# Attention with a mixture of experts on one core: the transposes between the second-layer products, and weight chunks in two DMAs

## The chip, the core and the metric

The kernel runs on one core of one Trainium2 chip. The metric is the device time of one execution in microseconds (us), as the median of several runs. Five engines work side by side, each on its own list of instructions: TensorE (PE) multiplies and transposes, VectorE (DVE), ScalarE (ACT) and GpSimd (POOL) do the elementwise work, and SyncE (SP) issues DMAs. They wait for one another by semaphores only.

## The reference

Block-causal attention over 8 batches of 8 heads, 576 rows and 64 columns, and then a layer of eight experts, of which each of the 4608 rows uses one.

```python
scores = scale * np.matmul(q, k.transpose(0, 1, 3, 2))
mask = block_i >= block_j                      # blocks of 64 rows
attn = softmax(np.where(mask, scores, -1e9))
x = np.matmul(attn, v)                         # rearranged to 4608 x 512

logits = x @ w_gate                            # 512 x 8
expert_idx = np.argmax(logits, axis=1)
gate_w = softmax(logits)[np.arange(N), expert_idx]
for e in range(E):                             # 8 experts
    mask = expert_idx == e
    h = np.maximum(x[mask] @ w1[e], 0.0)       # w1[e]: 512 x 1024
    out[mask] = gate_w[mask, None] * (h @ w2[e])   # w2[e]: 1024 x 512
```

All of it is float32. The kernel reaches that accuracy by splitting each operand into a high part and the rest and adding three products: high by high, rest by high, high by rest.

## The kernel before, in words

The first 370 us or so are attention with the routing behind it; the change doesn't touch them. The rest is the class `Experts`. The rows are sorted by expert into slots of 128 rows (38 of them here; three early slots, 0 to 2, are prepared before the others). A slot's way is:

- `gather(t)`: POOL issues an indirect DMA that fetches the slot's 128 rows into `xg`.
- `rows_in(t)`: PE transposes them, four 128 x 128 tiles, into `px` (L895). `rows_act(t)`: ACT copies `px` twice, to `xh` (rounded, L905) and to `xf` (L908). `rows_pool(t)`: POOL makes the rest `xl` (L914).
- `first_pe(t)`: 24 first-layer products (L936), 12 into each of the two banks `ph`; the second bank shows in the trace under the name `o`.
- The hidden rows of the two banks are transposed in two ways. For bank 0, ACT splits the 32-bit words into two planes of 16 bits (`planes`, L983), issues a DMA transpose (`turned`, L995), puts the planes together again when it has landed (`joined`, L1001), and applies the ReLU twice, to `hh` and to `h[0]` (`joined_high`, L1009 and L1010). For bank 1, ACT applies the ReLU (`relu_act(t,1)`, L974), PE transposes four tiles into `pt` (`hidden_pe(t,1)`, L1018), and ACT copies them twice (`hidden_act`, L1028 and L1031). POOL makes the rest of both (`hidden_low`, L1037).
- `second_pe(t, part)`: 24 second-layer products (L1057) into `py`, 12 in each part.
- `out_act(t)`: ACT scales the result by the gate (L1074), and `out_pool(t)`: POOL scatters it to the output by an indirect DMA (L1081).

`period(t)` is one turn of the loop, from slot 2 to slot 37. It is written once and gives every engine its instructions in this order; an engine takes only its own. On PE an ordinary turn is: `first_pe(t)`, `rows_in(t+1)`, `hidden_pe(t,1)`, then `second_pe(t-1, 0)` and `second_pe(t-1, 1)`. So the second layer of a slot runs one turn after its first. On ACT it is: `out_act(t-2)`, `planes(t)`, `turned(t)`, `relu_act(t,1)`, `rows_act(t+1)`, `hidden_act(t,1)`, `joined(t)`, `joined_high(t)`. On POOL: `out_pool(t-2)`, `gather(t+2)`, `rows_pool(t+1)`, `hidden_low(t,1)`, `hidden_low(t,0)`. `planes(t+1)` waits for `hidden_low(t,0)`, since both use `h[0]`.

The turn of slot 2 is different: there PE has all of slot 0's second layer (24 products) before `hidden_pe(2,1)`, and `rows_in(3)` with `rows_act(3)` stands between the two parts of slot 1's second layer, so that in ACT's list `rows_act(3)` comes behind `joined(2)` and `joined_high(2)`.

The weights of the next expert come while the present one works. SP loads chunks of 512 KB into five buffers `raw` (`load`, L1176): four chunks of w1, with 4 KB for each of 128 partitions, and four of w2, with two runs of 2 KB for each. Before a load beyond the fifth SP waits until DVE has used up the buffer. DVE splits each chunk into its high part (`high`, L1183) and its rest (`low`, L1189), four chunks at a time, when the buffer of the expert before last is free.

Of the kernel before, what the change touches and what calls it, by code (L numbers as in the profile page):

```python
# [18 lines left out]
P = 128  # L19
# [773 lines left out]
class Experts:  # L793
# [40 lines left out]
    def chunk(self, row, c):  # L834

        if c < 4:
            return self.w1.rearrange("e d f -> (e d) f")[bass.ds(row + P * c, P), :]
        w2 = self.w2.rearrange("e f d -> (e f) d")[bass.ds(row * 2 + 2 * P * (c - 4), 2 * P), :]
        return w2.rearrange("(k p) d -> p k d", p=P)

    def parts(self, e, c):

# [3 lines left out]
    def run(self):  # L846
        nc, tc, NS = self.nc, self.tc, self.nslot
        raw = self.raw
        nr = len(raw)
# [38 lines left out]
        def rows_in(t):  # L888

            if t >= EARLY:  # L890
                pe.wait_ge(sg[t % 4], 16 * gathered(t))
            if t >= 2:
                pe.wait_ge(sem["xa"], 2 * t - 2)
            for k in range(4):
                m = pe.transpose(self.px[:, P * k : P * k + P], self.xg[t % 4][:, P * k : P * k + P], self.ident)  # L895
                if t == 1 and k < 2:

                    m.then_inc(sem[("mm1", "mm2")[k]], (3, 1)[k])
            m.then_inc(sem["xt"], 1)
# [139 lines left out]
        def second_pe(t, part):  # L1039
            e8, off = self.regs[t]  # L1040
            todo = [
                (h[t % 2], base, c) for h, base in ((self.hh, 8192), (self.hl, 8192), (self.hh, 12288)) for c in range(8)
            ]
            if part == 0:
                pe.wait_ge(sem["wh"], e8 + 8 if t >= EARLY else 4)
                pe.wait_ge(sem["ha"], 4 * t + 3)
                if t >= 2:
                    pe.wait_ge(sem["ya"], t - 1)
            for n in range(12 * part, 12 * part + 12):
                h, base, c = todo[n]  # L1050
                if n == 8:
                    pe.wait_ge(sem["hp"], 2 * t + 2)
                if t == 0 and n >= 16 and c % 2 == 0:
                    pe.wait_ge(sem["wd"], 5 + c // 2)
                elif n == 16:
                    pe.wait_ge(sem["wd"], e8 + 8)
                m = pe.matmul(  # L1057
                    self.py[t % 2],
                    h[:, c // 4, P * (c % 4) : P * (c % 4) + P],
                    wf[:, bass.ds(off + (base + 512 * c), 512)],  # L1060
                    start=n == 0,
                    stop=n == 23,
                )
            if part == 1:
                m.then_inc(sem["mm2"], 1)
# [46 lines left out]
        def period(t):  # L1112
            more = t + 1 < NS
            if t > 2:
                first_pe(t)
                out_act(t - 2)
            planes(t)
            turned(t)
            relu_act(t, 1)
            if t == 2:  # L1120

                for f in range(2):
                    second_pe(0, f)
                out_act(0)
            elif more:
                rows_in(t + 1)
                rows_act(t + 1)
            hidden_pe(t, 1)
            hidden_act(t, 1)
            joined(t)  # L1130
            joined_high(t)
            for f in range(2):
                second_pe(t - 1, f)
                if t == 2 and f == 0:
                    rows_in(t + 1)
                    rows_act(t + 1)
            out_pool(t - 2)
            if t + 2 < NS:
                gather(t + 2)
            if more:  # L1140
                rows_pool(t + 1)
            for f in (1, 0):
                hidden_low(t, f, pool)
# [18 lines left out]
        with tc.tile_critical():  # L1162
            done = 0

            def do(m):

                nonlocal done
                done += 1
                m.then_inc(sem["do"], 1)
                dve.wait_ge(sem["do"], done)  # L1170

            def load(m, row):

                c = (m + 4) % 8
                dst = raw[m % nr] if c < 4 else raw[m % nr].rearrange("p (k d) -> p k d", k=2)
                sp.dma_start(dst, self.chunk(row, c)).then_inc(sraw[m % nr], 16)  # L1176

            def high(m):
                e, c = divmod(m + 4, 8)
                hi, _ = self.parts(e, c)  # L1180
                if m >= 4:
                    dve.wait_ge(sraw[m % nr], 16 * (m // nr + (m % nr == 4)))
                dve.tensor_copy(hi, raw[m % nr]).then_inc(sem["wh"], 1)  # L1183

            def low(m):
                e, c = divmod(m + 4, 8)
                hi, lo = self.parts(e, c)
                dve.wait_ge(sem["wh"], m + 5 if m >= 4 else 4)
                dve.tensor_sub(lo, raw[m % nr], hi).then_inc(sem["wd"], 1)  # L1189


            posi, g, cnt = self.router.rest
            last, t0 = self.router.B - 1, self.out.shape[0] - S
            sp.dma_start(
                self.router.by_partition(last, 3 * P, DM), self.y.rearrange("p (i c) -> p i c", c=P)
            ).then_inc(sem["ga"], 16)
            sp.dma_start(self.router.by_partition(last, GATE, GATE + 1), g[:, 0:4, None]).then_inc(sem["ga"], 16)
            sp.dma_start(self.xd[t0 : t0 + 64, GATE : GATE + 1], g[0:64, 4:5]).then_inc(sem["ga"], 16)
            begin()
            for i in range(5):  # L1200
                if i == 1:
                    rows_pool(1)
                self.router.scatter(last, i, posi).then_inc(sem["sc"], 16)
            rows_pool(2)
            gather(EARLY)
            for k in range(4):
                m = dve.tensor_copy(tuple(self.parts(0, k))[1], self.low[k].rearrange("p a b -> p (a b)"))
            m.then_inc(sem["lc"], 1)

            dve.wait_ge(sem["lc"], 1)  # L1210
            dve.sem_inc(sem["wd"], 4)
            for m in range(4):
                high(m)
            self.router.slots(cnt, do, self.bank)
            dve.sem_inc(sem["me"], 1)
            for f in range(2):
                hidden_low(0, f, dve)
            for f in range(2):
                low(2 * f)
                low(2 * f + 1)  # L1220
                hidden_low(1, f, dve)
            for f in range(2):
                o = slice(2048 * f, 2048 * f + 2048)
                dve.tensor_copy(self.w[:, 0, 0, o], self.high[:, o]).then_inc(sem["wh"], 2)
            sp.wait_ge(sem["sc"], 80)
            sp.dma_start(self.stab, self.router.tabv).then_inc(sem["st"], 16)

            sp.wait_ge(sem["me"], 1)
            sp.wait_ge(sem["mm1"], 2 * EARLY + 1)
            for e in range(1, E):  # L1230
                row = sp.value_load(self.row[e : e + 1, 0:1], min_val=0, max_val=DM * (E - 1))
                for c in range(8):
                    m = 8 * e + c - 4
                    if m >= nr:
                        sp.wait_ge(sem["wd"], m)
                    load(m, row)
                if e >= 2:
                    before = dve.value_load(self.before[e - 1 : e, 0:1], min_val=0, max_val=NS)
                for half, name, of in ((0, "mm1", lambda: before * 2 + 1), (4, "mm2", lambda: before + 1)):
                    if e >= 2:  # L1240
                        dve.wait_ge(sem[name], of())
                    for part in (high, low):
                        for c in range(half, half + 4):
                            part(8 * e + c - 4)
            total = None

            def tail(t):
                if t == NS:
                    finish(NS - 1)
                    return  # L1250
                with nc.If(total > t):
                    period(t)
                    tail(t + 1)
                with nc.Else():
                    finish(t - 1)

            for t in range(2, least):
                period(t)
            if least < NS:
                act.wait_ge(sem["me"], 1)  # L1260
                total = nc.values_load(self.before[E : E + 1, 0:1], min_val=0, max_val=NS)
                tail(least)
            else:
                finish(NS - 1)
# [129 lines left out]
```

## Time and profile before

| | us |
|---|---|
| median of 3 runs | 877.45 |
| lowest and highest run | 871.00, 880.23 |
| the profiled execution | 871.89 |
| its span in the trace | 870.1 |

The profile shows one execution, and its span is 1.8 us shorter than its time. An engine's busy time is that of its instructions; register, branch and semaphore work isn't counted. A line such as `L1018 PE MATMUL pt<-ident,h` names the line of the kernel, the engine, the operation, and the tile written and the tiles read. PEld is TensorE's loading of weights, which overlaps its products. ACTq and SPq are the DMA issues of ACT and SP. In a timeline the columns are the start, the duration of the group, engine, line, operation, and in brackets the idle time of the engine before it and what ended it.

The costliest groups of the page are these (busy us, then the mean ns of one, then the idle time before them):

```profile
L1057 PE MATMUL py<-w,low 128*128 (+1 forms) x912 | 224.2, 402 | 0.0
...
L936 PE MATMUL ph<-w,xh 128*128 x280 | 76.6, 396 | 2.1 <-ACT xh L905 2.1
L936 PE MATMUL o<-w,xh 128*128 x280 | 75.8, 393 | 0.0
```

The DMA issues of the weight chunks, with their size and the median time from issue to landing:

```profile
raw<-w SPq DMA_DIRECT2D x60, 512.0 KB, 5.3
```

Four of those 60 are loads of the first expert during attention, by another line; the other 56 are by `load`.

### The profile page before, as it was taken

The numbers are of one execution on the slowest core, as the hardware profiler recorded it, in microseconds if no ns is written. First come the engines' busy times: TensorE is split into PE (matmuls) and PEld (weight loads), VectorE is DVE, ScalarE is ACT, GpSimd is POOL, SyncE is SP. The second block draws the span as 40 slices with busy tenths as digits, with TensorE's granted clock in tenths as the row PEclk, the third lists the DMA queues.
The fourth block names the chain that finished last, engine by engine and source line by source line (L and its number), as shares of the span: only waits on it lengthen the run. The fifth ranks groups of instructions, "written<-read, shape, count | busy, mean of one in ns | idle before, by whom it ended". The sixth has DMA issues, their size and how long they took to land.

```text
span 870.1 us, 16492 instructions
## 1 busy us (share of the span) xinstructions
PE 825.4 (95%) x5126; PEld 633.9 (73%) x5126; DVE 425.8 (49%) x1208; ACT 555.1 (64%) x1254; POOL 352.4 (41%) x390
## 2 busy tenths in 40 slices
PE   5999999999999999998998999998998799999997
PEld 4777767777777777676876877786777577777775
DVE  5778787878787877478034000158256343000000
ACT  6889888888888888444554455444544444555453
POOL 2000223232323412445554545456556355554453
PEclk8999999999999999999999999999999899999999
DMA  5234748363635353528427422259557752122222
GB/s 196 96 112 152 153 130 168 118 157 114 148 116 142 107 132 122 129 53 262 154 74 173 132 59 74 74 134 249 155 147 225 170 138 70 48 74 74 59 51 64
DMA packets 83707, 108.81 MB, mean 125 GB/s; under 512 B 45601, under 2 KB 48929, under 8 KB 83618
## 3 DMA queue, kind: packets, MB, share of 16 engines
q1 hardware_dynamic: 38082, 78.26, 31.3%
q0 software_dynamic: 7520, 19.97, 7.9%
q10 hardware_dynamic: 38016, 9.44, 6.7%
q8 instruction: 50, 0.82, 0.4%
q14 instruction: 39, 0.32, 0.1%
HBM read 76.76 MB, written 21.98 MB: 113 GB/s over the span
## 4 chain that ended last, share of the span: by engine, by line
PE 77%; issue 6%; ACT 6%; POOL 2%; DMA 2%; ACTq 1%; POOLq 1%; DVE 1%; DVEq 0%
PE py L1057 20%; PE o L304 10%; PE ph L936 10%; PE o L936 9%; PE o L339 4%; PE ya L202 3%; PE xa L202 3%; PE pt L1018 2%; ACT h L974 2%; PE yb L202 2%; DMA kd<-kT 2%; ACTq L995 1%; PE o L333 1%; POOLq L1079 1%; ACT pb L234 1%
## 5 line engine op out<-in xcount | busy, mean ns | idle before, releaser
L1057 PE MATMUL py<-w,low 128*128 (+1 forms) x912 | 224.2, 402 | 0.0
L1057 PEld LDWEIGHTS py<-w,low 128*128 128x128 f32 x912 | 171.0, 191 | 37.7 <-issue 0.3
L1183 DVE CAST w<-raw 128x1024 fp32r<-128x1024 f32 x60 | 50.0, 880 | 206.8 <-PE o L936 154.3
L1037 POOL TENSOR_TENSOR low<-h,low 128x512 fp32r<-128x512 f32 x72 | 105.6, 1468 | 62.9 <-ACT h L1010 62.5
L247 POOL TENSOR_SCALAR p<-p,rs 128x64 f32<-128x64 f32 x32 | 14.2, 443 | 257.2 <-DVE rs L243 154.8
L1189 DVE TENSOR_TENSOR w<-raw,w 128x1024 fp32r<-128x1024 f32 x60 | 87.2, 1510 | 0.0
L914 POOL TENSOR_TENSOR xl<-xf,xh 128x512 fp32r<-128x512 f32 x38 | 51.1, 1346 | 86.6 <-ACT xf L908 86.4
L983 ACT COPY h<-ph 128x1024 uint16<-128x1024 uint16 x36 | 36.5, 1013 | 69.8 <-PE ph L936 61.3
L936 PE MATMUL ph<-w,xh 128*128 x280 | 76.6, 396 | 2.1 <-ACT xh L905 2.1
L936 PE MATMUL o<-w,xh 128*128 x280 | 75.8, 393 | 0.0
L1001 ACT COPY h<-hf 128x1024 uint16<-128x1024 uint16 x36 | 43.0, 1193 | 48.7 <-DMA hf<-h 48.5
L1081 POOL DMA_INDIRECT out<-y,idx x35 | 42.7, 1220 | 63.3 <-ACT y L1074 52.1
L936 PEld LDWEIGHTS ph<-w,xh 128*128 128x128 f32 x280 | 53.1, 190 | 14.6 <-issue 2.5
L974 ACT ACTIVATE h<-o 128x512 f32<-128x512 f32 x37 | 22.1, 598 | 63.4 <-PE o L936 54.7
L1074 ACT ACTIVATE y<-py,xg 128x512 f32<-128x512 f32 x38 | 26.1, 686 | 56.0 <-PE py L1057 54.5
L936 PEld LDWEIGHTS o<-w,xh 128*128 128x128 f32 x280 | 52.7, 188 | 11.7
L234 ACT ACTIVATE pb<-ya,neg 128x320 f32<-128x320 f32 (+2 forms) x93 | 48.6, 533 | 2.5 <-PE pt30x L273 1.8
L234 ACT ACTIVATE pb<-yb,neg 128x320 f32<-128x320 f32 (+2 forms) x93 | 49.5, 547 | 0.0
L731 POOL DMA_INDIRECT tab<-toks,posi x40 | 41.7, 1042 | 15.1 <-issue 14.6
L1018 PE MATMUL pt<-ident,h 128*128 128x128 f32 x152 | 25.1, 290 | 23.1 <-ACT h L974 23.1
L339 PE MATMUL o<-fold,oT 128*128 128x144 f32 x256 | 45.4, 300 | 0.9 <-ACT oT L311 0.6
L219 DVE TENSOR_REDUCE neg<-ya 128x1 f32<-128x320 f32 (+2 forms) x93 | 44.8, 482 | 0.8 <-ACT pb L234 0.8
(965 smaller groups left out, 2137.7 us busy)
## 6 DMA issues: line engine op xcount, KB each, us to landing
raw<-w SPq DMA_DIRECT2D x60, 512.0 KB, 5.3
qd<-qT SPq DMA_DIRECT2D x32, 352.0 KB, 3.0
v<-vt SPq DMA_DIRECT2D x32, 352.0 KB, 4.7
kd<-kT SPq DMA_DIRECT2D x32, 288.0 KB, 3.4
xd<-xt SPq DMA_DIRECT2D x7, 1026.0 KB, 11.6
xd<-xg SPq DMA_DIRECT2D x9, 256.5 KB, 6.5
xg<-w SPq DMA_DIRECT2D x8, 256.0 KB, 6.2
xd<-x SPq DMA_DIRECT2D x8, 128.0 KB, 6.2
```

Source lines behind the costliest of these rows:

```text
L202: ins = mm(out, q[x][r, 128 * (i - 1) : 128 * i], q[y][r, o : o + w], start=n == 0, stop=n == 2, skip_group_check=True,)
L219: ins = self.nc.vector.tensor_reduce(self.neg[m][:, c : c + 1], src, AX.XY if i == 4 else AX.X, ALU.max, negate=True)
L234: ins = self.nc.scalar.activation(dst, src, AF.Exp, bias=self.neg[m][:, c : c + 1], scale=1.0, accum_out=self.sums[m][:, c : c + 1])
L304: self.nc.tensor.matmul(out[r], self.raws[m][2][:, slot], self.ph[m, bank][:, c0:c1], start=t in (0, 5), stop=t in (4, 5), skip_group_chec ...
L339: mm(t[:, i], self.oT[m, 0][:, o : o + P], w, start=True, stop=True)
L914: pool.tensor_sub(self.xl, self.xf, self.xh).then_inc(sem["xp"], 1)
L936: m = pe.matmul(self.ph[f], x[:, P * k : P * k + P], weights(k, f, part), start=start and k == 0, stop=stop and k == 3,)
L1001: act.copy(self.h[0].bitcast(U16).rearrange("p (c o) -> p c o", o=2), self.hf.bitcast(U16).rearrange("p (o c) -> p c o", o=2),).then_inc(s ...
L1037: engine.tensor_sub(hl, self.hf if t < 2 else self.h[f], hh).then_inc(sem["hp"], 1)
L1057: m = pe.matmul(self.py[t % 2], h[:, c // 4, P * (c % 4) : P * (c % 4) + P], wf[:, bass.ds(off + (base + 512 * c), 512)], start=n == 0, st ...
L1183: dve.tensor_copy(hi, raw[m % nr]).then_inc(sem["wh"], 1)
L1189: dve.tensor_sub(lo, raw[m % nr], hi).then_inc(sem["wd"], 1)
```

## The change

Two things are changed. In `period`, the first part of the second-layer products of slot t-1 moves ahead of `rows_in(t+1)` and `hidden_pe(t,1)`, and the second part stays behind them, so that PE's eight transposes stand between the two parts. In the turn of slot 2 this puts `rows_in(3)` and `rows_act(3)` behind the first part of slot 1's second layer and ahead of `hidden_pe(2,1)` and `hidden_act(2,1)`.

In `load`, each chunk is taken as two halves of the columns, b = 0 and 1, each by its own DMA. The chunk is seen as 2 x 2 x 256 numbers for each partition, and a DMA carries two runs of 256 numbers (1 KB) for each. The bytes land where they did before. Each DMA adds 16 to the buffer's semaphore, so the count that DVE waits for is doubled.

```diff
     def chunk(self, row, c):
         if c < 4:
-            return self.w1.rearrange("e d f -> (e d) f")[bass.ds(row + P * c, P), :]
+            w1 = self.w1.rearrange("e d f -> (e d) f")[bass.ds(row + P * c, P), :]
+            return w1.rearrange("p (k b d) -> p k b d", k=2, b=2)
         w2 = self.w2.rearrange("e f d -> (e f) d")[bass.ds(row * 2 + 2 * P * (c - 4), 2 * P), :]
-        return w2.rearrange("(k p) d -> p k d", p=P)
+        return w2.rearrange("(k p) (b d) -> p k b d", p=P, b=2)
...
                 for f in range(2):
                     second_pe(0, f)
                 out_act(0)
-            elif more:
+            second_pe(t - 1, 0)
+            if more:
                 rows_in(t + 1)
                 rows_act(t + 1)
             hidden_pe(t, 1)
             hidden_act(t, 1)
             joined(t)
             joined_high(t)
-            for f in range(2):
-                second_pe(t - 1, f)
-                if t == 2 and f == 0:
-                    rows_in(t + 1)
-                    rows_act(t + 1)
+            second_pe(t - 1, 1)
             out_pool(t - 2)
...
             def load(m, row):
                 c = (m + 4) % 8
-                dst = raw[m % nr] if c < 4 else raw[m % nr].rearrange("p (k d) -> p k d", k=2)
-                sp.dma_start(dst, self.chunk(row, c)).then_inc(sraw[m % nr], 16)
+                dst, src = raw[m % nr].rearrange("p (k b d) -> p k b d", k=2, b=2), self.chunk(row, c)
+                for b in range(2):
+                    sp.dma_start(dst[:, :, b], src[:, :, b]).then_inc(sraw[m % nr], 16)
...
-                    dve.wait_ge(sraw[m % nr], 16 * (m // nr + (m % nr == 4)))
+                    dve.wait_ge(sraw[m % nr], 32 * (m // nr + (m % nr == 4)))
```

## The prediction

> **What bounds the kernel now.** I read the page first (span, busy time), then the list of waits of the expert stage, then the timeline of one ordinary turn of its loop, of a late turn and of the first turn, and last the DMA views.
>
> ```profile
> span 870.1 us, 16492 instructions
> ...
> PE 825.4 (95%) x5126; PEld 633.9 (73%) x5126; DVE 425.8 (49%) x1208; ACT 555.1 (64%) x1254; POOL 352.4 (41%) x390
> ```
>
> ```profile
> PE pt L1018 <- ACT h L974: 22.1, 35, 5.4
> ```
>
> PE is busy 95% of the span, so only its idle time and its slow time can go. The second fence is the list of waits from 404 us to the end: us in total, times, longest. Slots 3 to 37 are 35 turns, and in each one PE stands before `hidden_pe(t,1)` (L1018) because `relu_act` (L974) isn't done. No row there has PE waiting for a weight that DVE makes. An ordinary turn:
>
> ```profile
> 611.70 1.08 PE L936 MATMUL ph<-w,xh 128*128 x4
> ...
> 614.65 1.01 ACT L983 COPY h<-ph 128x1024 uint16<-128x1024 uint16 x1 [2.07 <-PE ph L936]
> ...
> 615.75 1.51 ACTq L995 DMA_TRANSPOSE hf<-h  x1
> ...
> 617.20 0.60 PE L895 MATMUL px<-ident,xg 128*128 128x128 f32 x4
> 617.40 0.60 ACT L974 ACTIVATE h<-o 128x512 f32<-128x512 f32 x1 [1.74 <-PE o L936]
> 617.89 0.58 ACT L905 CAST xh<-px 128x512 fp32r<-128x512 f32 x1
> ...
> 618.05 0.66 PE L1018 MATMUL pt<-ident,h 128*128 128x128 f32 x4 [0.25 <-ACT h L974]
> ...
> 618.46 5.83 PE L1057 MATMUL py<-w,low 128*128 x24
> ...
> 619.04 1.30 POOL L914 TENSOR_TENSOR xl<-xf,xh 128x512 fp32r<-128x512 f32 x1 [2.02 <-ACT xf L908]
> ...
> 622.45 1.17 ACT L1001 COPY h<-hf 128x1024 uint16<-128x1024 uint16 x1 [2.50 <-DMA hf<-h]
> ...
> 624.12 1.08 PE L936 MATMUL ph<-w,xh 128*128 x4
> 624.19 0.62 ACT L1010 ACTIVATE h<-h 128x512 f32<-128x512 f32 x1
> ...
> 624.88 1.31 POOL L1037 TENSOR_TENSOR low<-h,low 128x512 fp32r<-128x512 f32 x1 [3.28 <-ACT h L1010]
> ```
>
> The turn is 12.42 us (611.70 to 624.12): 5.50 of first-layer products, 0.85 from the px transposes to the pt transposes, 0.41 for pt, 5.66 of second-layer products. `relu_act` ends at 618.00 and pt starts at 618.05. Without a wait the same step is shorter, as the prologue shows:
>
> ```profile
> 379.94 0.60 PE L895 MATMUL px<-ident,xg 128*128 128x128 f32 x4
> ...
> 380.37 0.60 PE L1018 MATMUL pt<-ident,xg 128*128 128x128 f32 x4
> ```
>
> There it takes 0.43. So an ordinary turn loses 0.42, of which the list shows 0.25 (matmul ends are modelled).
>
> **Part one: the order on PE.** Twelve second-layer products of the slot before (half of 5.66, so 2.83 us) go between the first-layer products and the transposes. `relu_act` ends 6.30 after the turn's start (618.00 less 611.70); pt will be asked for at 5.50 + 2.83 + 0.44 = 8.77. The wait goes in every ordinary turn. Nothing is added to PE: the instructions are the same.
>
> The first and last of the 35 turns:
>
> ```profile
> 411.79 0.66 PE L1018 MATMUL pt<-ident,h 128*128 128x128 f32 x4 [0.25 <-ACT h L974]
> ...
> 851.94 0.66 PE L1018 MATMUL pt<-ident,h 128*128 128x128 f32 x4 [0.25 <-ACT h L974]
> ```
>
> 28 of the 35 are of 0.25; the other seven hold 22.1 - 28 x 0.25 = 15.1. The gross gain is 22.1 + 35 x 0.17 = **28.1 us**, if all are covered. The late ones come from the DMA transpose:
>
> ```profile
> 667.56 1.35 ACTq L995 DMA_TRANSPOSE hf<-h  x1
> ...
> 680.46 1.17 ACT L1001 COPY h<-hf 128x1024 uint16<-128x1024 uint16 x1 [8.70 <-DMA hf<-h]
> ...
> 687.07 0.60 ACT L974 ACTIVATE h<-o 128x512 f32<-128x512 f32 x1 [1.44 <-issue]
> ...
> 687.72 1.11 PE L1018 MATMUL pt<-ident,h 128*128 128x128 f32 x4 [5.37 <-ACT h L974]
> ```
>
> Here the transpose of 667.56 lands 12.9 later; from the end of `joined` (681.63) it is 6.1 us to pt, through `joined_high`, POOL's subtraction, `planes`, the next transpose's issue and `relu_act`. Before, `joined` had to end 0.15 ahead of the next turn (5.94 - 6.1), which allows a landing of 12.42 - 0.15 - 1.17 - 4.05 = 7.05 after the issue (4.05 is 615.75 less 611.70). After, it may end 8.77 - 6.1 = 2.67 into a next turn that comes at 12.0, which allows 9.4. So each late wait shrinks by some 2.4: only the two longest (5.37, and 3.23 below) survive, as 3.0 and 0.8.
>
> ```profile
> 591.64 0.66 PE L1018 MATMUL pt<-ident,h 128*128 128x128 f32 x4 [3.23 <-ACT h L974]
> 592.05 7.38 PE L1057 MATMUL py<-w,low 128*128 x24
> ```
>
> ```profile
> 688.49 7.05 PE L1057 MATMUL py<-w,low 128*128 x24
> ```
>
> ```profile
> 592.00:595.80 3.80, 3.80 (x13) 2.98 (x12) 1.36 (x3) 1.53 (x4) 3.50 (x4) 0.55 1.10 194
> ```
>
> These two waits also cost speed: the 24 products behind them take 7.38 and 7.05 against 5.83, and the granted clock is 0.55 from 592.0 to 595.8. That is 1.55 + 1.22 = **2.8 us**, gone if the waits are. The Trainium skill, "TensorE: Matmul & The Clock Gate", section "Part 1: The HAM clock gate", halves the clock after an idle window of about 3.4 us; by that rule a remaining 3.0 could keep the clock, and the sum would be 1.2 lower than where it is lost again. The trace agrees with the size (0.55 after an idle 3.23).
>
> What is queued behind the moved steps: on ACT, `rows_act(t+1)` now waits until px is done at about 9.0 into the turn, and behind it stand `hidden_act`, `joined` and `joined_high`. By the spacings of the ordinary turn (617.89 to 622.45 without the 2.50 of waiting, then 1.74 to L1010, 0.62, and 1.31 of POOL) POOL's last subtraction ends at about 14.8. The next `planes` falls due at 12.0 + 2.95 (614.65 less 611.70) = 14.95, just in time, and it may be some 2.4 late before PE sees it, as worked out above. xh is ready at 9.6 and needed at 12.0; xl at 9.0 + 1.15 + 1.30 = 11.45 and needed at 12.0 + 0.92. Those are the next things to be late: xl's cover is 1.4 us. The gather that px needs gets 2.83 more room.
>
> **Part two: the first turn.** There the px transposes and `rows_act(3)` move ahead of `hidden_pe`, and in ACT's queue ahead of `joined(2)`, which waits for a DMA.
>
> ```profile
> 387.76 5.83 PE L1057 MATMUL py<-w,low 128*128 128x512 f32 x24
> ...
> 397.86 0.60 PE L895 MATMUL px<-ident,xg 128*128 128x128 f32 x4
> ...
> 400.17 1.18 ACT L1001 COPY h<-hf 128x1024 uint16<-128x1024 uint16 x1 [3.81 <-DMA hf<-h]
> ...
> 402.43 0.57 ACT L905 CAST xh<-px 128x512 fp32r<-128x512 f32 x1
> ...
> 403.35 1.20 PE L936 MATMUL ph<-w,xh 128*128 x4 [2.09 <-ACT xh L905]
> ...
> 410.94 0.60 PE L895 MATMUL px<-ident,xg 128*128 128x128 f32 x4
> ```
>
> px is done by 398.5, but xh comes at 402.43 because `joined(2)` and `joined_high(2)` stand ahead of it; then slot 3 runs slowly (403.35 to 410.94, 7.59 against 5.50). After: 387.76 + 5.66 + 2.83 + 0.85 (px and pt) + 2.83 = 399.93 for slot 3's start, and 405.43 for its end instead of 410.94: **5.5 us**. If that start still waits for something, the slow clock may stay: then 3.4.
>
> **Part three: the weight DMAs.** 56 chunks of 512 KB come by 112 DMAs, with runs of 1 KB instead of 4 KB (first layer) and 2 KB (second).
>
> ```profile
>   ACT h L1001: 48.5, 15
> ...
> DMA to landing us min/median/max: 3.1/4.1/12.9
> ```
>
> ```profile
> q1 hardware_dynamic: 38082, 78.26, 31.3%
> ...
> q10 hardware_dynamic: 38016, 9.44, 6.7%
> ```
>
> ```profile
> DVE w L1183 <- DMA raw<-w: 6.2, 6, 2.4
> ```
>
> Mean packet time is the share times 16 engines times 870.1 us over the packets: q1, which carries the weights, 114 ns for 2,055 bytes; q10, the transposes, 24.5 ns for 248. On the line between, a run of 1 KB takes an estimated 63 ns, so an engine's 32 runs of a chunk take 2.0 us against 1.8 for 2 KB. The weights land a little later, for which DVE would wait; it waits 6.2 us for them now, off PE's path, and the second issue stands in SP's queue with only the next chunk behind it. What counts is the transposes, one a turn: ACT waits for 15 of them, 48.5 us. If their packets take turns with those of the weights, each waits a shorter time behind a run of half or a quarter the length. Bounds: all landings under 9.4 leave nothing of the late waits (0); the seven late turns all at the worst row, 12.9, leave 3.0 + 1.2 each (29). The row nearest to a turn is what it has now: 3.8 + 1.2 = 5.0. I take half of that, **2.4**, since shorter turns on the engines should help.
>
> Two rules bear on it. The Trainium skill, "DMA: Bandwidth & Descriptors", section "Queues, rings and completion order", says that an engine goes round its queues packet by packet; by that the late waits vanish and the sum is 2.4 lower, which the landings of up to 12.9 beside weight traffic support. Its section "Rules for kernel authors" speaks against the change: gather small transfers into large ones, 1 MiB or more. By its sentence the split only costs; that is the third rival.
>
> **Sum.** 28.1 + 2.8 + 5.5 - 2.4 = 34.0 off the profiled execution's 871.89 is 837.9. That execution is 5.6 below the median of 877.45; if what the others have more is late waits of this kind, it goes too, and if it lies in the attention half it stays. I carry half: **841 us**.
>
> **Rivals.**
> 1. The DMA part doesn't do what it is made for: landings stay. Then 2.6 more, about 843. For it: the transposes also share with gathers and with the output, which don't change.
> 2. POOL's xl takes the place of the ReLU. It has 1.4 us of cover, and beside DVE's work one subtraction is longer:
>
> ```profile
> 606.62 2.38 POOL L914 TENSOR_TENSOR xl<-xf,xh 128x512 fp32r<-128x512 f32 x1 [0.41 <-ACT xf L908]
> ```
>
> At 2.38 instead of 1.30 the cover is still 0.3; a late gather issue in front of it, say 1 us in the 15 turns in which ACT waits for the DMA, gives 15 us: 856. Against it: DVE is idle in most turns.
> 3. Smaller runs lengthen the transfers. The seven late turns go to the worst row: 871.9 - 36.4 + 29 = 865, with some of it 856 to 866.
> 4. The other side, slower: the same at every one of the 15 turns that wait for a transpose. Each loses 4.2, 63 in all, against 36.4: 871.9 + 27 = 899, or 904 by the median. It decides from 36.4 / 15 = 2.4 a turn, which is a landing near 11.8 in all of them. Against it: only the longest of the landings reaches 12.9, and an estimated 0.2 us more for a chunk's runs is far from that.
>
> **How the numbers follow.** Forecast 0.50 (841), first rival 0.28 (843), POOL 0.08 (850 to 856), longer transfers 0.10 (855 to 868), slower 0.04. The forecast and the first rival spread from 832 (all waits gone is 835.5, and the runs shown lie up to 6.5 below their median) to 850; the range to 858 takes in POOL's case and leaves the longer transfers partly out. About 1% (8.8 us) is what a measurement can tell from no change. Faster by more than that, below 868.7: 0.92; within: 0.04; slower: 0.04.
>
> **What would show it.** In the list of waits, L1018 on L974 falls from 22.1 to under 5, and the ordinary turn from 12.42 to 12.0. Slot 3 starts near 400, about 3.4 us earlier. The slow-clock stretches near 592 and 688 are gone. The transposes' longest landing falls under 9.4, while the q1 packets grow in number by 18,000 (28,672 runs of 1 KB, where 28 chunks had 128 runs and 28 had 256). Wrong would be a new row of PE waiting for L914 (second rival), for L1037 or the weights, or a landing median above 5 (third and fourth).

## The result and the profile after

| | us |
|---|---|
| before, median of 4 runs (lowest, highest) | 876.04 (871.00, 880.23) |
| changed, median of 4 runs (lowest, highest) | 836.83 (835.89, 838.61) |
| ratio, with its 95% interval | 0.9557 (0.9502 to 0.9613) |
| the profiled execution of the changed kernel, and its span | 836.29, 834.6 |

The change makes the kernel 4.4% faster, and its runs lie within 2.7 us of each other where those of before spread over 9.2. Ratios, here and below, leave out runs that lie more than 1.5% above the fastest of the same kernel. The page of the changed kernel:

```profile
PE 814.5 (98%) x5126; PEld 632.2 (76%) x5126; DVE 421.2 (50%) x1208; ACT 554.5 (66%) x1254; POOL 352.9 (42%) x390
```

PE is busy for 98% of a span that is 35.5 us shorter, with the same 5126 products and transposes. Its line numbers have moved by one: L1018 of before is L1019, L1057 is L1058. The list of waits from 404 us on (total us, times, longest):

```profile
ACT h L984 <- POOL low L1038: 19.5, 12, 2.6
...
DVE w L1182 <- DMA raw<-w: 14.0, 9, 5.1
ACT h L1002 <- DMA hf<-h: 6.9, 4, 3.3
...
PE pt L1019 <- ACT h L975: 1.2, 2, 1.0
```

The 22.1 us that PE waited for the ReLU are 1.2. Two waits have grown off PE's path: `planes` on ACT waits for POOL in 12 turns (19.5 us, 8.5 before), and DVE waits for weights (14.0 us, 7.0 before). An ordinary turn in the timeline:

```profile
593.63 1.08 PE L937 MATMUL ph<-w,xh 128*128 x4
...
597.68 1.25 ACTq L996 DMA_TRANSPOSE hf<-h  x1
...
598.96 1.69 POOL L878 DMA_INDIRECT xg<-xd,idx  x1 [0.27 <-POOL idx L874]
599.13 2.96 PE L1058 MATMUL py<-w,low 128*128 x12
599.34 0.60 ACT L975 ACTIVATE h<-o 128x512 f32<-128x512 f32 x1 [1.74 <-PE o L937]
601.93 0.60 PE L896 MATMUL px<-ident,xg 128*128 128x128 f32 x4
...
602.37 0.60 PE L1019 MATMUL pt<-ident,h 128*128 128x128 f32 x4
...
605.59 1.10 PE L937 MATMUL ph<-w,xh 128*128 x4
```

The turn is 11.96 us (593.63 to 605.59) instead of 12.42. The ReLU ends at 599.94, and pt follows px by 0.44 with no wait in brackets. The first turn:

```profile
387.96 8.61 PE L1058 MATMUL py<-w,low 128*128 128x512 f32 x36
...
396.41 0.60 PE L896 MATMUL px<-ident,xg 128*128 128x128 f32 x4
...
397.05 0.59 ACT L906 CAST xh<-px 128x512 fp32r<-128x512 f32 x1 [1.85 <-PE px L896]
...
400.07 1.10 PE L937 MATMUL ph<-w,xh 128*128 x4
...
402.16 1.18 ACT L1002 COPY h<-hf 128x1024 uint16<-128x1024 uint16 x1 [3.06 <-DMA hf<-h]
```

xh now comes ahead of `joined(2)` (L1002), and slot 3 starts at 400.07 without a wait, though the transpose lands late.

### The profile page after: what moved, and what is told of

The parts are those of the page before. It is cut to its first block, busy times and chain, and to the rows that moved or that the text cites. A ratio compares the mean times of both kernels' runs of the same rounds, so it can differ in the third digit from the quotient of the medians.

```text
span 834.6 us, 16660 instructions
## 1 busy us (share of the span) xinstructions
PE 814.5 (98%) x5126; PEld 632.2 (76%) x5126; DVE 421.2 (50%) x1208; ACT 554.5 (66%) x1254; POOL 352.9 (42%) x390
## 4 chain that ended last, share of the span: by engine, by line
PE 85%; ACT 3%; issue 3%; POOL 2%; DMA 2%; DVE 1%; POOLq 1%; ACTq 0%; DVEq 0%
PE py L1058 22%; PE ph L937 11%; PE o L937 11%; PE o L304 10%; PE o L339 4%; PE ya L202 3%; PE xa L202 3%; PE yb L202 2%; PE px L896 2%; PE pt L1019 2%; DMA kd<-kT 2%; ACT pb L234 2%; PE o L333 1%; POOL low L1038 1%; PE o L190 1%
## 5 line engine op out<-in xcount | busy, mean ns | idle before, releaser
L1058 PE MATMUL py<-w,low 128*128 (+1 forms) x912 | 226.9, 398 | 0.8 <-ACT low L1010 0.8
L1058 PEld LDWEIGHTS py<-w,low 128*128 128x128 f32 x912 | 168.8, 188 | 38.1 <-issue 1.2
L1188 DVE TENSOR_TENSOR w<-raw,w 128x1024 fp32r<-128x1024 f32 x60 | 81.8, 1420 | 0.0
L906 ACT CAST xh<-px 128x512 fp32r<-128x512 f32 x38 | 22.3, 587 | 87.7 <-PE px L896 87.7
L1082 POOL DMA_INDIRECT out<-y,idx x35 | 36.8, 1052 | 40.3 <-issue 36.3
L1002 ACT COPY h<-hf 128x1024 uint16<-128x1024 uint16 x36 | 43.3, 1202 | 10.1 <-DMA hf<-h 10.0
L878 POOL DMA_INDIRECT xg<-xd,idx x37 | 44.4, 1200 | 10.3 <-POOL idx L874 10.3
L731 POOL DMA_INDIRECT tab<-toks,posi x40 | 41.8, 1044 | 15.1 <-issue 14.3
L219 DVE TENSOR_REDUCE neg<-ya 128x1 f32<-128x320 f32 (+2 forms) x93 | 44.7, 481 | 1.5 <-ACT pb L234 1.5
```

Of the source, the lines that this page charges most:

```text
L219: ins = self.nc.vector.tensor_reduce(self.neg[m][:, c : c + 1], src, AX.XY if i == 4 else AX.X, ALU.max, negate=True)
L878: pool.indirect_dma_start(out=self.xg[i], out_offset=None, in_=self.xd[:, :], in_offset=bass.IndirectOffsetOnAxis(ap=self.idx[:, t : t + 1 ...
L1058: m = pe.matmul(self.py[t % 2], h[:, c // 4, P * (c % 4) : P * (c % 4) + P], wf[:, bass.ds(off + (base + 512 * c), 512)], start=n == 0, st ...
```

## The experiments

Each run is compared with the kernel before on the same chip. "Old order" and "new order" are PE's orders before and after the change.

**One part at a time.** The first kernel has the diff of `period` alone, the second the diff of `chunk`, `load` and `high` alone.

> The new order on PE, the weight DMAs as before. Theory A (the order and the shorter runs each do a part): the ordinary turn falls from 12.42 to 12.0 us and the first turn's 5.5 us go, but transposes still land up to some 13 us late beside weights; 3 to 5 us of waits at L1018 remain, so 841 to 845. Rival N (the order does it all, the DMA part nothing): 837, as with both.

> The weight DMAs of the change, the order on PE as before. Theory A: outside the first turn no transpose lands later than 7 us, so the seven late waits (13.4 us above the ordinary 0.25) and the slow clock behind two of them (2.8) go and the ordinary waits stay: about 860, with some 9 us left at L1018. Rival N: 876, as before, with 22 us at L1018.

Measured: the order alone 837.60 us (ratio 0.9567, 0.9484 to 0.9649), the DMA part alone 876.52 (1.0006, 0.9939 to 1.0073). The order alone gives the whole gain that can be measured, as rival N had it. In the list of waits, first with the DMA part alone, then with the order alone (where no row of PE waiting for the ReLU is left):

```profile
ACT h L1002 <- DMA hf<-h: 39.5, 13, 6.0
...
PE pt L1019 <- ACT h L975: 20.2, 35, 6.1
```

```profile
ACT h L1001 <- DMA hf<-h: 6.2, 6, 1.9
```

Theory A falls in both halves. With runs of 1 KB in the old order ACT still waits 39.5 us for transposes (44.7 before, from 404 us on), and with the old long runs in the new order only 6.2. So the transposes became short with the order, not with the runs of 1 KB.

**Two DMAs without the runs of 1 KB.** Both in the old order:

```diff
-sp.dma_start(dst[:, :, b], src[:, :, b])      # e2: runs of 1 KB
+sp.dma_start(dst[:, b], src[:, b])            # e3: one run of 2 KB a partition
...
+h = slice(64 * b, 64 * b + 64)                # e4: halves of the partitions,
+sp.dma_start(dst[h], src[h])                  #     runs of 4 and 2 KB
```

> Old order; two DMAs a chunk, but each with one run of 2 KB for a partition (first-layer chunks from 4 to 2 KB, second-layer chunks keep their 2 KB). If the length of the runs matters: a part of the gain, 864 to 872, with landings still above 7 us where second-layer chunks come. If the number of DMAs matters: all of it, 860, as with runs of 1 KB.

> Old order; two DMAs a chunk, by halves of the partitions, with the runs of before (4 and 2 KB). If the length of the runs matters: no change, 874 to 878, landings up to some 13 us. If the number of DMAs matters: 860, landings under 7 us.

Measured: 883.77 us (1.0066, 1.0036 to 1.0096) and 883.45 (1.0103, 1.0038 to 1.0168). Neither is faster, and the transposes are not short: ACT waits for them 45.9 and 42.7 us from 404 us on (44.7 before). By the ratios, splitting a chunk costs 0.7% and 1.0% here; by the medians of all runs (878.86 for the kernel before on this chip) it is 0.6% and 0.5%. With runs of 1 KB no cost shows.

**Are the weights behind the late waits at all?** No loads from the third expert in use on, in the old and in the new order:

```diff
-                    load(m, row)
+                    if e < 2:
+                        load(m, row)
...
-                if m >= 4:
+                if 4 <= m < 12:
                     dve.wait_ge(sraw[m % nr], ...)
```

> The kernel before, without the weight loads from the third expert in use on (DVE converts what lies in the buffers, so the output is not the reference's). Theory W: the late waits come from weight traffic beside the transposes; without it the seven late waits (13.4 us above the ordinary 0.25) and the slow clock (2.8) go: 860 to 863, about 9 us left at L1018, and no landing above 7 us after the first turn. This is the most that any form of the weight DMAs could bring in the old order. Rival P: they come from the gathers, the outputs and POOL's slowness beside DVE: 874 or more, 18 us or more at L1018.

> The changed kernel without the same loads (the output is not the reference's). If the new order hides all of the weight traffic: 835 to 837, nothing gained. If the runs of 1 KB still cost or the traffic still delays PE: 833 or less.

Old order: 858.77 us (0.9838, 0.9755 to 0.9922). The list of waits:

```profile
PE pt L1018 <- ACT h L974: 8.8, 35, 0.3
```

All 35 waits are ordinary ones (35 x 0.25 = 8.8). Theory W holds: without the loads the late waits are gone, so no late wait comes about without the weight traffic. About 859 us is then also the best time that any form of the weight DMAs could have given the old order.

New order: 852.06 us (0.9773, 0.9677 to 0.9869), 15 us slower than with the loads. That fits neither expectation. The timeline shows one place:

```profile
579.16 2.49 DVE L1182 CAST w<-raw 128x1024 fp32r<-128x1024 f32 x4
...
580.60 13.66 POOL L915 TENSOR_TENSOR xl<-xf,xh 128x512 fp32r<-128x512 f32 x1 [2.77 <-ACT xf L909]
...
581.57 4.62 DVE L1188 TENSOR_TENSOR w<-raw,w 128x1024 fp32r<-128x1024 f32 x4
...
586.11 2.49 DVE L1182 CAST w<-raw 128x1024 fp32r<-128x1024 f32 x4
588.52 4.62 DVE L1188 TENSOR_TENSOR w<-raw,w 128x1024 fp32r<-128x1024 f32 x4
...
594.32 2.07 PE L937 MATMUL ph<-w,xl 128*128 x4 [10.77 <-POOL xl L915]
```

POOL's xl, elsewhere 1.3 us, takes 13.66: it ends at 594.26, 1.1 us behind DVE's last conversion, and PE waits 10.77 for it, of the 13.2 us by which the two profiled executions differ. Behind the wait the granted clock is 0.51 from 594.3 to 597.6. Without loads to wait for, DVE converts three groups of four chunks without a break, 24 operations from 570.73 to 593.14. That alone doesn't hold POOL up: without the loads in the old order DVE also does 24 operations without a break, from 582.62 to 610.38, and two xl beside them take 1.66 and 1.47 us. The first of the two:

```profile
589.58 5.82 DVE L1183 CAST w<-raw 128x1024 fp32r<-128x1024 f32 x4
589.77 1.66 POOL L914 TENSOR_TENSOR xl<-xf,xh 128x512 fp32r<-128x512 f32 x1 [1.51 <-ACT xf L908]
```

Here DVE is the one that is slowed: its four casts take 5.82 us, against 2.49 above. What decides between the two cases isn't shown; the long hold-up was seen once.

**The issue of the transpose, and the gather.** What differs around a transpose is seen first in a late turn of before (first fence) and the same turn with the new order alone:

```profile
457.82 1.49 SPq L1176 DMA_DIRECT2D raw<-w  x2
...
459.10 0.99 POOL L877 DMA_INDIRECT xg<-xd,idx  x1 [0.27 <-POOL idx L873]
459.23 2.45 ACTq L995 DMA_TRANSPOSE hf<-h  x1
...
469.64 1.18 ACT L1001 COPY h<-hf 128x1024 uint16<-128x1024 uint16 x1 [5.31 <-DMA hf<-h]
```

```profile
450.76 2.60 SPq L1173 DMA_DIRECT2D raw<-w  x2
...
454.09 1.01 ACT L983 COPY h<-ph 128x1024 uint16<-128x1024 uint16 x1 [2.41 <-POOL low L1037]
...
455.18 1.34 ACTq L995 DMA_TRANSPOSE hf<-h  x1
456.54 0.99 POOL L877 DMA_INDIRECT xg<-xd,idx  x1 [0.27 <-POOL idx L873]
...
461.57 1.18 ACT L1001 COPY h<-hf 128x1024 uint16<-128x1024 uint16 x1 [0.77 <-DMA hf<-h]
```

Before, the transpose is issued while SP issues the last load of a burst (457.82 to 459.31) and 0.13 behind a gather, the issue itself takes 2.45 us, and the copy that waits for it starts 10.4 later. In the new order `planes` waits for POOL, so the transpose comes 1.8 us behind the last load's issue (which ends at 453.36) and 1.4 ahead of the gather, and the copy starts 6.4 later. The gather stands behind the transpose in every turn of the new order, by 1.1 us or more, also where loads are issued right beside it. But the latest transpose of before, at 667.56, landing 12.9 us later, has its gather 0.9 us behind it (668.44), so the gather ahead can't be all. Two kernels in the old order move one of these at a time:

```diff
-            turned(t)
             relu_act(t, 1)
+            turned(t)                 # e11
...
-            if t + 2 < NS:
-                gather(t + 2)
             if more:
                 rows_pool(t + 1)
+            if t + 2 < NS:            # e12
+                gather(t + 2)
```

> The kernel before, with ACT's issue of the DMA transpose moved behind relu_act, some 2 us later in the turn; the weight DMAs stay. Theory C (a transpose issued just behind the last of a burst of weight loads waits for that burst; the new order helped because it issues it later): the longest landings after the first turn fall from 13 to under 8 us, the transpose's issue no longer takes up to 2.4 us, and the time falls to 860 to 868. Rival B (the transposes share the DMA engines with the burst whenever they come): landings stay at 9 us and more, and the later issue adds to them: 876 to 885.

> The kernel before, with POOL's gather of the rows of slot t+2 moved behind the subtraction xl of slot t+1, so that it is issued some 3 us or more behind the DMA transpose and not just ahead of it; the weight DMAs and PE's order stay. Theory G (in the old order the late turns have the gather 0.1 us ahead of the transpose; in the new order it comes 1 to 2.5 us behind, and the transposes are short though the weights are the same): the longest landings after the first turn fall under 8 us, L1018's waits to 9 to 12 us, 860 to 866. Rival L (weight loads alone make a transpose late): landings of 9 us and more remain, 874 or more.

The later issue came out slower, at 899.01 us (1.0220, 1.0000 to 1.0439, an interval that reaches down to no change). In its late turns the transpose mostly lies behind the output and the gather, and landings reach 15.1 us. The list of waits, of the slowest of its four runs (907.68 us):

```profile
ACT h L1001 <- DMA hf<-h: 86.2, 20, 11.7
...
PE pt L1018 <- ACT h L974: 37.0, 35, 6.0
```

So theory C in its simple form falls, and the landings are as rival B had them, with a time above both. The later gather gave 867.98 us (0.9943, 0.9892 to 0.9995), with the waits at

```profile
PE pt L1018 <- ACT h L974: 13.3, 35, 3.4
```

instead of 22.1, a part of what theory G asked for, and between the times of theory G and rival L. Both lists are of one execution each. And one turn has a late transpose with the gather 5 us behind it:

```profile
612.41 21.16 SPq L1176 DMA_DIRECT2D raw<-w  x6
...
612.97 1.25 ACTq L995 DMA_TRANSPOSE hf<-h  x1
...
613.43 1.96 POOL L1081 DMA_INDIRECT out<-y,idx  x1 [3.48 <-issue]
...
617.96 1.00 POOL L877 DMA_INDIRECT xg<-xd,idx  x1 [0.27 <-POOL idx L873]
625.76 1.18 ACT L1001 COPY h<-hf 128x1024 uint16<-128x1024 uint16 x1 [8.59 <-DMA hf<-h]
```

So the weight loads are needed for a late transpose; a gather just ahead of it seems to add to it, but isn't needed. In this turn a burst of loads begins 0.6 us ahead of the transpose and the output is issued 0.5 behind it; whether the loads can do it alone isn't shown. Which of the spacings decides stays open.

**The first turn.** In the changed kernel, the turn of slot 2 back in its old order:

```diff
-            second_pe(t - 1, 0)
-            if more:
-                rows_in(t + 1)
-                rows_act(t + 1)
+            if t > 2:
+                second_pe(t - 1, 0)
+                if more:
+                    rows_in(t + 1)
+                    rows_act(t + 1)
             hidden_pe(t, 1)
             hidden_act(t, 1)
             joined(t)
             joined_high(t)
+            if t == 2:
+                second_pe(t - 1, 0)
+                rows_in(t + 1)
+                rows_act(t + 1)
             second_pe(t - 1, 1)
```

> The changed kernel, with the turn of slot 2 alone in its old order. The prediction's second part gave the first turn 5.5 us: then 842. Rival: what the first turn gains is made up for later, 837, as the changed kernel.

Measured 843.84 us (841.61 to 845.64), 7.0 above the changed kernel. Slot 3 then waits for xh again:

```profile
406.53 1.69 PE L937 MATMUL ph<-w,xh 128*128 x4 [3.38 <-ACT xh L906]
```

Behind this wait the granted clock is 0.50 from 407.0 to 413.8, 6.8 us, where the kernel before has 0.50 from 404.4 to 407.8, 3.4 us. That would make the loss larger than the 5.5 forecast.

**How many products go ahead.** In the changed kernel, the split 12 and 12 becomes 4 and 20, 20 and 4, 24 and 0:

```diff
-            for n in range(12 * part, 12 * part + 12):
+            for n in (range(4) if part == 0 else range(4, 24)):   # or 20; 24: both parts ahead
```

> The changed kernel with 4 second-layer products ahead of the transposes instead of 12. pt is asked for at 5.50 + 4 x 0.236 + 0.44 = 6.88 us into the turn, and relu_act ends at 6.30: the ordinary wait stays covered. A landing may be 7.05 + 0.94 - 0.42 = 7.6 us. If landings stay below that in the new order: 836 to 839. If the late waits need the full 2.83 us of cover: 842 to 846, with waits of 3 us or more in all at L1019.

> The changed kernel with 20 second-layer products ahead of the transposes. px starts at 5.50 + 20 x 0.236 = 10.22, and POOL's xl ends 3.14 us behind px's start (617.20 to 620.34 in the trace of before): 13.36, against 12.92, when the next turn's first layer asks for it. By that 0.44 us a turn, 35 turns, 15 us: 850 to 854, and PE waits for POOL's xl. Rival: xl is ready sooner than worked out, 837.

> The changed kernel with all 24 second-layer products ahead of the transposes. px starts at 11.16, xh is ready at 12.43 against 12.0, and xl at 14.30 against 13.35: 0.43 + 0.95 us a turn, 35 turns, 48 us: 880 to 890, as slow as before the change. Rival, that the order matters only for the ReLU's wait: 837.

Measured: 837.36 us with 4 ahead (834.27 to 844.42), 859.86 with 20 (858.54 to 861.50), and 891.56 with 24 (ratio to before 1.0169, 1.0110 to 1.0229). In the lists of waits, for 4, 20 and 24:

```profile
PE pt L1019 <- ACT h L975: 3.8, 2, 2.7
```

```profile
PE ph L937 <- POOL xl L915: 12.2, 34, 1.2
```

```profile
PE ph L937 <- ACT xh L906: 15.3, 29, 0.6
...
PE ph L937 <- POOL xl L915: 13.7, 34, 0.5
```

With 4, only two waits of the ReLU remain and the median is that of 12, though one run is 7 us above it. With 20, xl becomes what PE waits for in nearly every turn, and with 24 xh and xl, as their cover was worked out. Both cost somewhat more than expected (860 against 850 to 854, 892 against 880 to 890). The lists show only about half of what these kernels lose to the changed one (12.2 of 23 us, 29.0 of 55), as they showed 0.25 of 0.42 us for the ReLU. None of these beats the changed kernel.

## Why the prediction was right, and where it was not

The forecast was 841 in 832 to 858, and the median is 836.83. The sum for the profiled execution was 837.9; it took 836.29. The order was right in mechanism, term by term; the DMA part was not, and the small size of its term kept that from showing in the number.

- **The ordinary turn**: predicted 12.0, measured 11.96. The gross gain of 28.1 was the waits (22.1, of which 1.2 are left) and the 0.17 a turn that the list doesn't show; the turn is 0.46 shorter, where 0.42 was forecast.
- **The slow clock** behind two long waits (2.8) is gone with them: the page's clock row stands at 9 through this stage but for its last slice, and the mean granted clock is 0.995 against 0.987.
- **The first turn**: predicted 5.5. From slot 0's second layer to the end of slot 3's first layer it was 23.18 us (387.76 to 410.94) and is 17.71 (387.96 to 405.67), 5.47 less:

```profile
405.67 2.96 PE L1058 MATMUL py<-w,low 128*128 128x512 f32 x12
```

- **What is late next**: xl and then xh were named, with a cover of 1.4 us for xl. With 20 products ahead xl is what PE waits for, with 24 both are.
- **The DMA part** is the step that failed. I took half of the 5.0 us that might remain, "since shorter turns on the engines should help". They did not help in the old order (1.0006), and in the new order there was nothing to help: with the order alone no wait for the ReLU is left. The premise behind it was wrong too. I took a turn's landings under the new order to be "what it has now", and they got shorter: after the first turn the longest is 6.6 us with the order alone and 7.2 with both changes, 12.9 before. The gather that now comes behind the transpose is a likely part of the cause; the whole cause stays open. Of the term of 2.4 the list shows 1.2, and not where it was expected: the turns near 592 and 688 have no wait left, and the 1.2 stands in the turns of slots 3 and 4, behind the first turn's landing of 9.6 us and the next one of 7.2. So the forecast that all landings would fall under 9.4 just missed.
- **The first rival**, that the DMA part doesn't do what it is made for, was true and cost nothing, since it was priced with the landings as they were.
- **The two rules** of the Trainium skill, "DMA: Bandwidth & Descriptors": from its engines taking turns packet by packet (section "Queues, rings and completion order") I concluded that runs of 1 KB would help; no run here shows that. Its advice to make one large transfer of small ones (section "Rules for kernel authors") fits e3 and e4, by the 0.7% and 1.0% above, while e2 shows no cost.
- **The carried half** of the 5.6 between the profiled execution and the median should have been nothing: the changed kernel's median is 0.5 above its profiled execution. What the other runs of before had more seems to have been late waits; that is argued from the spread, not shown.

## What to carry to other kernels

Where the engine that bounds a loop waits for a short step of another engine, look for work of the same engine that depends on neither, and put just enough of it in between; then work out what the delayed steps feed, since moving 20 instead of 12 products made the next operand late in nearly every turn. A reordering moves the issue of DMAs too, and with it their collisions, so a part of a change that is aimed at a collision has to be measured with and without the new order. A mean of the waits doesn't show this; the rows of one late turn beside the same turn in the other kernel do.

## What the runs showed of the hardware

A GpSimd subtraction of 128 x 512 numbers, 1.3 us alone, was once held up for 13.66 us beside VectorE operations that followed each other without a break, the last 14 of 24, and ended about 1 us behind the last of them. In the changed kernel, with the loads, the longest xl is 1.76 us:

```profile
L915 POOL TENSOR_TENSOR xl<-xf,xh x38: 1287/1297/1761, 375.2 to 819.2; 128x512 fp32r<-128x512 f32 x38
```

The Trainium skill, "SBUF — State Buffer", section "SBUF: two separate sides", says that VectorE and GpSimd share a pair of ports that one instruction holds alone from its start to its end. The trace agrees that one can shut the other out, but there it lasted over 14 instructions and not one; beside the 24 operations of the other kernel without the loads neither shut the other out (xl 1.66 us, four casts 5.82). The hold-up cost more than leaving the transfers out could bring.
